# Logits of a unit's first block moved into the next unit, last scaling split in thirds, branch order changed, in a fused WKV and two-layer expert kernel

## The chip, the cores and the metric

The kernel runs as one launch on one core of a Trainium2 chip. The metric is the device time of the launch in microseconds (us), the median of the runs shown. A measurement of this kernel tells a change from none at about 0.5%.

## The reference

An attention part (a recurrence over 768 positions, two batches, eight heads of 48) makes 1536 tokens of 384 numbers. Two expert layers follow, each with 8 experts of width 1024. In both a token goes to the expert with the largest logit, and its result is scaled with that expert's softmax weight:

```
logits = x @ w_gate (+ modality bias, layer 0 alone)
e      = argmax(logits);  gate = softmax(logits)[e]
out    = gate * (relu(x @ w1[e]) @ w2[e])
```

Layer 1 reads layer 0's output. It also drops tokens beyond a capacity per expert. Its logits, `x @ w_gate` of layer 0's output, are made inside layer 0 as each block of results is finished.

## The kernel before, in words

**Units.** After the attention, `routing` sorts the tokens by expert into blocks of 128 and pairs the blocks into units of 256 with one expert each. `moe` then runs unit after unit: `body(j)` for j = 0 to 5 always, then `rest(j)`, which branches on the number of units that there are. With these inputs layer 0 has 8 units and layer 1 has 10. A unit with two blocks runs `two(j, pc)`, one with a single block runs `one(j, pc)`; `body` chooses with a branch on a register, `kd`, which every engine loads for itself. The form that stands second in the branch is reached by a jump.

**Work of a unit.** All products are made in three passes of float32r parts (high by high, high by low, low by high). `first2` makes a quarter of the hidden layer (18 matmuls of 256 columns, lines 1106), ScalarE and VectorE split it into `hh` and `hl` (lines 1111, 1112); `second2` adds a quarter to the output of one block (6 matmuls of 384 columns, line 1124). Between these stand `split` calls: ScalarE casts the next unit's weights to a high part (`hi`, line 965) and VectorE takes the low part (`lo`, line 968), ten pieces in all. `xprep` transposes the next unit's tokens (line 1024) and splits them (lines 1025, 1026). `gates` makes the softmax weight: part 0 on VectorE (lines 1033, 1034), part 1 an exponential on ScalarE (line 1036), part 2 on VectorE (1039, 1040). `scale(j, t)` multiplies the output of block t by it (line 1132).

**Logits of layer 0's output.** `yturn3` transposes a scaled block (line 1145), `ysplit3` splits it into three bf16 parts in the one buffer `yp` (1147 to 1152), and `ylog3` makes the logits with nine matmuls of 24 columns (line 730), reduces them (731) and stores the block with an indirect DMA. Of units 1 to 7 block 0's logits end the unit itself: `yturn3(j, 0)` stands between `second2(1, 1)` and `second2(2, 1)`, `ylog3(j, 0)` behind `second2(3, 1)`. Of unit 0 they stand in unit 1. Block 1's logits are made in the following unit.

**Order.** The order is written out by hand (`manual_schedule`); every engine runs its queue in program order, and its sequencer, which waits, loads registers and branches, runs ahead of it as far as no wait stops it. Inside `one` the order comes from the strings `ONE`: each letter is a step (a to j a piece of weights, y, z, l the logits of the block before, 0 and 1 the relus, Q part 2 of the gates, s the last scaling).

**End of layer 0.** `last(7)` is reached by a jump over the code of units 8 to 12. It transposes the last block (`yturn`, line 694), copies it, makes its logits (line 704), adds them to the logits that the other blocks stored, and layer 1's `routing` begins. While no product can run, `warm` keeps TensorE busy with matmuls of constants, 512 columns each (line 762): lists of 4 and 12 in the routing, 2 behind it, then 15 and 4 around the first unit's transposes.

Of the kernel before, what the change touches and what calls it, by code (L numbers as in the profile page):

```python
# [9 lines left out]
F32 = mybir.dt.float32  # L10
# [18 lines left out]
P = 128  # L29
# [14 lines left out]

WARM = (4, 12, 2, 15, 4)
TP = (3, 4)
OHP = ((0, 6), (6, 10), (10, 12))
# [21 lines left out]
SCALE = 'ssv'  # L69
LATE = (1,)  # L70
RELU = "sv"
PB = (1, 3, 1, 2)
ONE = (('ecadfyz', '01bQ', 'X', 'l', 'hgix', 'js'), ('badec0', 'f1hQ', 'xX', 'i', 'j', 'g'))

# [614 lines left out]

def turn3(tc, c, ap, psum, xt, n, tag, bufs):  # L690
    nc = tc.nc
    pt = psum.tile([P, KD, P], F32, tag=tag, name="lpt" + n, bufs=bufs)
    for kc in range(KD):
        nc.tensor.transpose(pt[:, kc], xt[:, kc * P : (kc + 1) * P], c.ident)
    xT = ap.tile([P, KD, P], F32, tag="lxT", name="lxT" + n, bufs=1)
    nc.scalar.copy(xT, pt)
    return [xT[:, kc] for kc in range(KD)]


def logits(tc, psum, xT, wg, dst, bias, n, tag, bufs):  # L700
# [58 lines left out]

def warm(nc, c, ps, k):  # L760
    for _ in range(k):
        nc.tensor.matmul(ps, lhsT=c.ones, rhs=c.i1.rearrange("p a b -> p (a b)")[:, 0:512].bitcast(BF16), start=True, stop=True)


def routing(tc, c, g, rp, layer, lg, cap, best, run, pick=None, bad=None, inside=None):
# [4 lines left out]
    with ExitStack() as ctx:  # L770
# [17 lines left out]
        pw = bank("warm0", "h", [P, 512])  # L788
        warm(nc, c, pw, WARM[0])
        nc.tensor.matmul(pc[:, 1], lhsT=c.blk, rhs=tot, start=False, stop=True, skip_group_check=True)  # L790
        nc.tensor.matmul(pc[:, 0], lhsT=c.tri, rhs=tot, start=True, stop=True, skip_group_check=True)
        warm(nc, c, pw, WARM[1])

# [48 lines left out]
        for col in range(NC):  # L842
            nc.tensor.matmul(pid, lhsT=ohp[:, :, col], rhs=rid[:, col], start=(col == 0), stop=(col == NC - 1))
        warm(nc, c, pw, WARM[2])
        R.ids = rp.tile([P, NB], I32, name="ids" + n)
# [89 lines left out]
class MoePools:  # L935
    def __init__(self, tc, ctx, raw, run):
        self.cp = cp = ctx.enter_context(tc.tile_pool(name="mo_c" + run, bufs=1, reuse_waits="tile"))
        self.ap = ctx.enter_context(tc.tile_pool(name="mo_p" + run, bufs=2, reuse_waits="tile"))

        def slots(nm, shape, dt, k=2):  # L940
            return [cp.tile(shape, dt, name=f"{nm}{i}") for i in range(k)]

        self.raw = raw
        self.w1r, self.w2r = raw.w1r, raw.w2r
        self.w1h = slots("w1h", [P, KD, F], F32R)
        self.w1l = slots("w1l", [P, KD, F], F32R)
        self.w2h = slots("w2h", [P, KF, DM], F32R)
        self.w2l = slots("w2l", [P, KF, DM], F32R)
        self.xg = slots("xg", [P, 2, XW], F32)
        self.xh = slots("xh", [P, KD, U], F32R)  # L950
        self.xl = slots("xl", [P, KD, U], F32R)
        self.yo = slots("yo", [P, 2, XW], F32)
        self.yp = cp.tile([P, 3, KD, P], BF16, name="yp")
        tc.nc.gpsimd.memset(self.yp, 0.0)
        self.gd = slots("gd", [P, 2, E + 1], F32)
        self.gm = cp.tile([P, 2, 2], F32, name="gm")


def moe(tc, c, m, route, run, layer, src, w1d, w2d, dst, wg2, wp2, zb, following, lgs=None, psum=None, bad=None, general=None, ykeep=None):
# [21 lines left out]
    with ctx:  # L981
# [133 lines left out]
        def second2(j, q, t, between=None):  # L1115
            s = j % 2
            hh, hl = st["t", j, q]
            if q == 0:
                st["y", j, t] = ykeep[t]
            ts = slice(t * P, t * P + P)  # L1120
            i = 0
            for (a, w) in ((hh, m.w2h), (hh, m.w2l), (hl, m.w2h)):
                for f in range(2):
                    nc.tensor.matmul(st["y", j, t], lhsT=a[:, f, ts], rhs=w[s][:, 2 * q + f], start=(q == 0 and i == 0), stop=(q == 3 and i == 5))  # L1124
                    i += 1
                    if i == 2 and between:
                        between()

# [28 lines left out]

        def yturn(j, t):
            st["yT", j, t] = turn3(tc, c, ap, psum, m.yo[j % 2][:, t], f"_y{j}{t}" + n, "tp", TP[layer])

        def ylog(j, t, out=True):
            pl = logits(tc, psum, st.pop(("yT", j, t)), wg2, m.yo[j % 2][:, t, DM:XW] if out else None, None, f"_y{j}{t}" + n, "lg", 1)
            if out:
                store(j, t)
            return pl

        def own(j, k):
# [11 lines left out]
        def one(j, pc):  # L1179
# [3 lines left out]
            def work():  # L1183
                for p in next(plan):
# [3 lines left out]
                    elif p == "y":  # L1188
                        if before:
                            if j == 1:  # L1190
                                ylog3(0, 0)
                            yturn3(j - 1, 1)
# [3 lines left out]
                    elif p == "l":  # L1196
                        if before:
                            ylog3(j - 1, 1)
                    elif p == "Q":
                        gates(j, 2)  # L1200
                    elif p == "s":
                        if layer == 0:
                            scale(j, 1, "s")
# [31 lines left out]
        def two(j, pc):  # L1235
            before = layer == 0 and j > 0
            first2(j, 0)
            if before:
                if j == 1:
                    ylog3(0, 0)  # L1240
                yturn3(j - 1, 1)
                ysplit3()
            own(j, 0)
            if j or layer:
# [13 lines left out]
            if j or layer:  # L1258
                split(pc, 6, 10)
            else:  # L1260
                split(pc, 3, 6)
            second2(j, 0, 1)
            first2(j, 3)
            if j == layer == 0:
                split(pc, 6, 8)
            second2(j, 1, 0)
            second2(j, 2, 0)
            if layer == 0:
                second2(j, 3, 0)
                scale(j, 0, SCALE[1])  # L1270
            if j + 1 < NU:
                for t in range(2):
                    xprep(j + 1, t)
            if layer:
                second2(j, 3, 0)
                scale(j, 0, SCALE[1])
            if j == layer == 0:
# [5 lines left out]

            second2(j, 1, 1)
            if layer == 0 and j:
                turned()
            second2(j, 2, 1)
            second2(j, 3, 1, turned if j == layer == 0 else None)
            if layer == 0:
                if j:  # L1290
                    ylog3(j, 0)
                scale(j, 1, "s")

        def body(j):
            pc = pieces(m, j + 1) if j + 1 < NU else []
            gates(j, 0)
            gates(j, 1)
            loads(j + 2)
# [8 lines left out]
            if j and layer:  # L1307
                finish(j - 1)
            if layer == 0 and j == NU_MIN - 1:

# [14 lines left out]
        for i in range(6) if layer == 0 else ():  # L1325
            lo(p0[i], nc.vector)
        warm(nc, c, psum.tile([P, 512], F32, tag="h", name="warm" + n, bufs=2), WARM[3])
        st["k"] = kind(0)
        xprep(0, 1)
        warm(nc, c, psum.tile([P, 512], F32, tag="h", name="warm1" + n, bufs=2), WARM[4])  # L1330
        for kc in range(KD):
# [8 lines left out]
        def last(j):  # L1340
            if layer:
                finish(j)
            else:
# [11 lines left out]
                m.raw.load(j % 2, *following, slice(er, er + 1), parts=(1,))  # L1355
                yturn(j, 1)
                py = ylog(j, 1, False)
                nc.vector.tensor_tensor(put, py.unsqueeze(1).to_broadcast((P, NC, E)), ohc.unsqueeze(2).to_broadcast((P, NC, E)), ALU.mult)
# [151 lines left out]
```

## Time and profile before

| what | value |
|---|---|
| median of three runs | 459.4 us (457.96 to 459.79) |
| the profiled execution's own time | 457.46 us |
| its span, first to last instruction | 455.4 us |
| TensorE busy (matmul) | 420.0 us, 92% of the span |
| VectorE busy | 330.4 us, 73% |
| ScalarE busy | 248.2 us, 55% |
| GpSimd busy | 142.6 us, 31% |
| mean granted TensorE clock | 0.985 |

The attention takes the first 112 us or so of the span, layer 0 runs from there to about 278, layer 1 to the end. Busy shares are means over all of it. A row of the timeline gives start and length in us, engine, line, operation and operands, how many were merged (x), and in brackets how long the engine was idle before it and which engine's signal ended that. Matmuls are pipelined: a merged row lasts longer than it holds up the next, which then starts before the row's end.

### The profile page before, as it was taken

What the parts mean: (1) busy time and instruction counts of PE and PEld (TensorE: products, weight loads), DVE (VectorE), ACT (ScalarE), POOL (GpSimd) and SP (SyncE); (2) the same over time, 40 slices, a digit from 0 to 9 for tenths busy, and PEclk for the clock granted to TensorE, in tenths of its full rate; (3) what the DMA queues carried; (4) which work ended last, traced back from release to release, by engine and by line L of the source; (5) the groups of instructions that cost most, each with busy time, mean ns of one, the idle gap of its engine ahead of it and who ended that gap; (6) DMA issues with size and microseconds to landing.
All of it is one profiled execution on the core that took longest, in us unless ns stands there. A gap on an engine that the chain in (4) does not pass through costs nothing. (4 is left out here: it accounts for less than half of the span.)

```text
span 455.4 us, 9522 instructions
## 1 busy us (share of the span) xinstructions
PE 420.0 (92%) x3212; PEld 376.5 (83%) x3212; DVE 330.4 (73%) x677; ACT 248.2 (55%) x504; POOL 142.6 (31%) x158
## 2 busy tenths in 40 slices
PE   8999999998899999999898976999899999998990
PEld 4789988886399989899897863699799999997990
DVE  7798777984888948677686895487874945868760
ACT  3356545544456646556374670277754755777650
POOL 5647953150330321212232220503343123124420
PEclk9999999999999999999999997999999999999997
DMA  5996247268520230357652855304886656762100
GB/s 113 197 157 132 52 80 197 43 223 304 172 73 2 72 94 19 108 159 243 215 185 64 304 188 157 89 21 142 285 285 248 240 185 232 234 223 55 46 22 19
DMA packets 85588, 66.95 MB, mean 147 GB/s; under 512 B 60586, under 2 KB 77655, under 8 KB 85504
## 3 DMA queue, kind: packets, MB, share of 16 engines
q1 hardware_dynamic: 80512, 52.30, 39.0%
q0 software_dynamic: 4992, 13.61, 9.4%
q8 instruction: 42, 0.69, 0.6%
q14 instruction: 42, 0.34, 0.2%
HBM read 95.63 MB, written 11.56 MB: 235 GB/s over the span
## 5 line engine op out<-in xcount | busy, mean ns | idle before, releaser
L968 DVE TENSOR_TENSOR w1l<-w1r,w1h 128x512 fp32r<-128x512 f32 x114 | 71.8, 686 | 13.7 <-ACT w1h L965 13.7
L968 DVE TENSOR_TENSOR w2l<-w2r,w2h 128x768 fp32r<-128x768 f32 x76 | 68.3, 951 | 0.1
L965 ACT CAST w1h<-w1r 128x512 fp32r<-128x512 f32 x114 | 62.8, 619 | 1.3 <-issue 1.0
L1112 DVE SCALAR_TENSOR_TENSOR qhl_m<-qh_m,qhh_m 128x512 fp32r<-128x512 f32 x48 | 32.9, 686 | 39.4 <-ACT qhh_m L1111 39.4
L965 ACT CAST w2h<-w2r 128x768 fp32r<-128x768 f32 x76 | 58.3, 834 | 0.0
L1106 PE MATMUL qh_m<-xh,w1h 128*128 128x256 f32 x288 | 51.4, 287 | 3.4 <-ACT yo L1132 3.1
L1106 PE MATMUL qh_m<-xl,w1h 128*128 128x256 f32 x288 | 50.3, 283 | 0.9 <-DVE w2l L968 0.7
L1124 PE MATMUL y_m<-w2h,qhh_m 128*128 128x384 f32 x192 | 50.4, 344 | 0.0
L1124 PE MATMUL y_m<-w2h,qhl_m 128*128 128x384 f32 x192 | 49.6, 339 | 0.8 <-DVE qhl_m L1112 0.7
L1106 PE MATMUL qh_m<-xh,w1l 128*128 128x256 f32 x288 | 49.8, 282 | 0.0
L1124 PE MATMUL y_m<-w2l,qhh_m 128*128 128x384 f32 x192 | 49.2, 337 | 0.0
L1111 ACT ACTIVATE qhh_m<-qh_m 128x512 fp32r<-128x512 f32 x48 | 28.7, 598 | 33.3 <-PE qh_m L1106 33.3
L1137 POOL DMA_INDIRECT x<-yo,ids_l x14 | 17.3, 1236 | 93.7 <-ACT w2h L965 33.1
L1009 POOL DMA_INDIRECT xg<-x,idg_l x24 | 24.6, 1025 | 69.4 <-DVE gd L1034 44.5
L1106 PEld LDWEIGHTS qh_m<-xh,w1h 128*128 128x128 f32 x288 | 42.3, 188 | 4.2 <-ACT yo L1132 3.4
L1106 PEld LDWEIGHTS qh_m<-xl,w1h 128*128 128x128 f32 x288 | 41.0, 188 | 1.5 <-DVE w2l L968 1.1
L1132 ACT ACTIVATE yo<-y_m,gate_l 128x384 f32<-128x384 f32 x30 | 17.5, 582 | 43.1 <-PE y_m L1124 40.1
L1106 PEld LDWEIGHTS qh_m<-xh,w1l 128*128 128x128 f32 x288 | 40.9, 188 | 0.0
L1137 POOL DMA_INDIRECT out_dram<-yo,ids_l x20 | 24.1, 1203 | 49.5 <-ACT w1h L965 13.9
L1124 PEld LDWEIGHTS y_m<-w2h,qhl_m 128*128 128x128 f32 x192 | 34.4, 188 | 2.4 <-DVE qhl_m L1112 2.4
L1009 POOL DMA_INDIRECT xg<-xs,idg_l x20 | 22.0, 1102 | 43.7 <-issue 21.1
L395 ACT ACTIVATE X<-endt,Sb 112x112 f32<-112x112 f32 x40 | 14.2, 354 | 38.2 <-PE endt L385 27.2
(250 smaller groups left out, 868.7 us busy)
## 6 DMA issues: line engine op xcount, KB each, us to landing
w2r<-in_moe_w_dram SPq DMA_DIRECT2D x50, 768.0 KB
w1r<-in_moe_w_dram SPq DMA_DIRECT2D x72, 512.0 KB
xs<-zv SPq DMA_DIRECT2D x12, 192.0 KB
out_dram<-zt SPq DMA_DIRECT2D x4, 576.0 KB
raw_w<-in_w_dram SPq DMA_DIRECT2D x14, 144.0 KB
raw_r<-in_r_dram SPq DMA_DIRECT2D x14, 144.0 KB
raw_k<-in_k_dram SPq DMA_DIRECT2D x14, 144.0 KB
raw_v<-in_v_dram SPq DMA_DIRECT2D x14, 144.0 KB
```

Of the source, the lines that this page charges most:

```text
L395: nc.scalar.activation(Xn, z, AF.Identity, scale=Tn)
L965: (eng.copy if eng is nc.scalar else eng.tensor_copy)(p[1], p[0])
L968: eng.tensor_sub(p[2], p[0], p[1].bitcast(F32))
L1009: nc.gpsimd.indirect_dma_start(out=m.xg[j % 2][:, t], out_offset=None, in_=src, in_offset=bass.IndirectOffsetOnAxis(ap=R.idg[:, 2 * j + t ...
L1106: nc.tensor.matmul(ph[:, f], lhsT=w[s][:, kc, fs], rhs=a[s][:, kc], start=(i == 0), stop=(i == 3 * KD - 1))
L1111: nc.scalar.activation(hh, ph, AF.Relu)
L1112: nc.vector.scalar_tensor_tensor(hl, ph, 0.0, hh.bitcast(F32), ALU.max, ALU.subtract)
L1124: nc.tensor.matmul(st["y", j, t], lhsT=a[:, f, ts], rhs=w[s][:, 2 * q + f], start=(q == 0 and i == 0), stop=(q == 3 and i == 5))
L1132: nc.scalar.activation(m.yo[j % 2][:, t, 0:DM], py, AF.Identity, scale=R.gate[:, 2 * j + t : 2 * j + t + 1])
L1137: nc.gpsimd.indirect_dma_start(out=dst, out_offset=bass.IndirectOffsetOnAxis(ap=R.ids[:, 2 * j + t : 2 * j + t + 1], axis=0), in_=m.yo[j % ...
```

## The change

- `two`: of units 0 to 4 (`NU_MIN` is 6) block 0 is transposed inside `second2(2, 1)`, behind its second matmul, and `ylog3(j, 0)` moves to the following unit, behind `first2(0)`. From unit 5 on it is transposed inside `second2(1, 1)` behind the fourth matmul, and `ylog3` stands inside `second2(3, 1)` behind the fourth. In layer 0 `xprep` moves ahead of `second2(3, 0)`, as it was in layer 1. The tenth piece of weights is split behind `first2(3)`.
- Part 1 of the gates moves from `body` into the forms: behind `first2(0)` in `two`, letter P in `one`.
- The scaling of block 1 moves out of `two` and `one` for units 5 and up of layer 0, into `body(j + 1)` ahead of its branch, or into `last`, where it is made in three parts of 128 columns, each with its own transposition and copy.
- The form `one` stands first in the branch for units 6 and 7 and no longer for unit 5.
- Three of the five `warm` lists run in layer 1 as four times as many matmuls of 128 columns.
- Block 0 of both buffers `yo` is cleared once on GpSimd, before layer 0.

```diff
+WIDE = ((512, 512, 512, 512, 512), (512, 512, 128, 128, 128))
+ONE_FIRST = (6, 7)
-ONE = (('ecadfyz', '01bQ', 'X', 'l', 'hgix', 'js'), ('badec0', 'f1hQ', 'xX', 'i', 'j', 'g'))
+ONE = (('ecadfPyz', '01bQ', 'X', 'l', 'hgix', 'js'), ('badec0P', 'f1hQ', 'xX', 'i', 'j', 'g'))
...
+def warm(nc, c, ps, i, layer):
+    w = WIDE[layer][i]
+    for _ in range(WARM[i] * 512 // w):
+        nc.tensor.matmul(ps[:, 0:w], lhsT=c.ones, rhs=c.i1.rearrange("p a b -> p (a b)")[:, 0:w].bitcast(BF16), start=True, stop=True)
...
+        for x in self.yo:
+            tc.nc.gpsimd.memset(x[:, 0], 0.0)
...
-                            if j == 1:
-                                ylog3(0, 0)
+                            if j < NU_MIN:
+                                ylog3(j - 1, 0)
...
                     elif p == "s":
-                        if layer == 0:
+                        if layer == 0 and j < NU_MIN - 1:
                             scale(j, 1, "s")
...
+            gates(j, 1)
             own(j, 0)
...
-                split(pc, 6, 10)
+                split(pc, 6, 9)
...
+            else:
+                split(pc, 9, 10)
             second2(j, 1, 0)
             second2(j, 2, 0)
-            if layer == 0:
-                second2(j, 3, 0)
-                scale(j, 0, SCALE[1])
             if j + 1 < NU:
                 for t in range(2):
                     xprep(j + 1, t)
-            if layer:
-                second2(j, 3, 0)
-                scale(j, 0, SCALE[1])
+            second2(j, 3, 0)
+            scale(j, 0, SCALE[1])
...
-            second2(j, 1, 1)
-            if layer == 0 and j:
-                turned()
-            second2(j, 2, 1)
-            second2(j, 3, 1, turned if j == layer == 0 else None)
-            if layer == 0:
-                if j:
-                    ylog3(j, 0)
+            end = layer == 0 and j >= NU_MIN - 1
+            second2(j, 1, 1, (turned, 4) if end else None)
+            second2(j, 2, 1, (turned, 2) if layer == 0 and not end else None)
+            second2(j, 3, 1, (lambda: ylog3(j, 0), 4) if end else None)
+            if layer == 0 and not end:
                 scale(j, 1, "s")
...
             gates(j, 0)
-            gates(j, 1)
...
             if j and layer:
                 finish(j - 1)
-            if layer == 0 and j == NU_MIN - 1:
+            elif j >= NU_MIN:
+                scale(j - 1, 1, "s")
+            if layer == 0 and j in ONE_FIRST:
...
-                yturn(j, 1)
-                py = ylog(j, 1, False)
+                for kc in range(KD):
+                    ks = slice(kc * P, kc * P + P)
+                    nc.scalar.activation(m.yo[j % 2][:, 1, ks], ykeep[1][:, ks], AF.Identity, scale=R.gate[:, col])
+                xT = ap.tile([P, KD, P], F32, tag="lxT", name=f"lx{j}" + n, bufs=1)
+                for kc in range(KD):
+                    pt = psum.tile([P, P], F32, tag="h" if kc == 1 else "tp", name=f"yt{j}{kc}" + n, bufs=2 if kc == 1 else TP[0])
+                    nc.tensor.transpose(pt, m.yo[j % 2][:, 1, kc * P : (kc + 1) * P], c.ident)
+                    nc.scalar.copy(xT[:, kc], pt)
+                py = logits(tc, psum, [xT[:, kc] for kc in range(KD)], wg2, None, None, f"_y{j}1" + n, "lg", 1)
```

## Rows read from the trace of the kernel before

**Rows 1.** Waits of TensorE, 120 to 290 us: total us, times, longest.
```profile
PE qh_m L1106 <- ACT yo L1132: 3.1, 4, 1.0
PE hp_m L1077 <- DVE h_m L1070: 1.6, 2, 1.0
PE hp_m L1077 <- ACT h_m L1068: 1.5, 1, 1.5
PE ph_m L1058 <- ACT yo L1132: 1.2, 1, 1.2
```
**Rows 2.** Timeline, TensorE, the end of unit 1.
```profile
163.35 0.51 PE L1124 MATMUL y_m<-w2h,qhl_m 128*128 128x384 f32 x2
163.70 0.52 PE L730 MATMUL l_y_m<-wp,yp 128*128 128x24 bf16 x9
164.96 0.36 PE L1106 MATMUL qh_m<-xh,w1h 128*128 128x256 f32 x1 [0.74 <-ACT yo L1132]
```
**Rows 3.** Timeline, TensorE and ScalarE, the end of unit 0.
```profile
144.07 0.52 PE L1106 MATMUL qh_m<-xh,w1h 128*128 128x256 f32 x3
145.15 0.39 PE L1106 MATMUL qh_m<-xl,w1h 128*128 128x256 f32 x1 [0.20 <-DVE yp L1151]
...
144.27 0.58 ACT L1132 ACTIVATE yo<-y_m,gate_l 128x384 f32<-128x384 f32 x1 [0.16 <-PE y_m L1124]
```
**Rows 4.** TensorE's branches of `body`, 163.6 to 165.1, then 141 to 144 us.
```profile
L1316 PEldq COMPARE_BRANCH  x2: 65/176/286, 164.0 to 164.7; - x2
...
L1316 PEldq COMPARE_BRANCH  x2: 65/192/319, 141.2 to 142.0; - x2
```
**Rows 5.** Timeline, TensorE and VectorE, unit 2's last quarter.
```profile
178.81 0.52 PE L1124 MATMUL y_m<-w2l,qhh_m 128*128 128x384 f32 x2
179.53 0.62 PE L1124 MATMUL y_m<-w2h,qhl_m 128*128 128x384 f32 x2 [0.20 <-DVE qhl_m L1112]
...
176.19 2.69 DVE L968 TENSOR_TENSOR w2l<-w2r,w2h 128x768 fp32r<-128x768 f32 x3
```
**Rows 6.** Timeline, ScalarE and VectorE, the start of unit 7.
```profile
260.44 0.22 ACT L1036 ACTIVATE gd<-gd 128x16 f32<-128x16 f32 x1 [0.96 <-DVE gd L1034]
261.28 1.14 ACT L965 CAST w1h<-w1r 128x512 fp32r<-128x512 f32 x2 [0.62 <-issue]
...
261.99 0.69 DVE L968 TENSOR_TENSOR w1l<-w1r,w1h 128x512 fp32r<-128x512 f32 x1 [1.58 <-ACT w1h L965]
```
**Rows 7.** Timeline, ScalarE and TensorE, the end of layer 0.
```profile
270.83 0.84 ACT L965 CAST w2h<-w2r 128x768 fp32r<-128x768 f32 x1
272.58 0.58 ACT L1132 ACTIVATE yo<-y_m,gate_l 128x384 f32<-128x384 f32 x1 [0.91 <-PE y_m L1093]
275.31 0.48 ACT L696 COPY lxT_y_m<-lpt_y_m 128x384 f32<-128x384 f32 x1 [2.15 <-DVE sp_m L1350]
...
275.84 1.45 PE L704 MATMUL lpl_y_m<-wg,lxT_y_m 128*128 128x8 f32 x6 [1.84 <-ACT lxT_y_m L696]
```
**Rows 8.** TensorE's branch into `last`, 269 to 276 us; then all of the span.
```profile
L1380 PEldq COMPARE_BRANCH  x1: 3407/3407/3407, 269.8 to 269.8; - x1
...
L1380 PEldq COMPARE_BRANCH  x10: 65/66/4684, 246.1 to 446.0; - x10
```
**Rows 9.** The page's groups: ScalarE's scaling of 112 columns, in the attention.
```profile
L395 ACT ACTIVATE X<-endt,Sb 112x112 f32<-112x112 f32 x40 | 14.2, 354 | 38.2 <-PE endt L385 27.2
```
**Rows 10.** Timeline, TensorE: layer 1's warm matmuls and transposes; nine short matmuls.
```profile
286.44 3.40 PE L762 MATMUL warm_m<-i,ones 128*128 128x512 bf16 x15
289.68 0.49 PE L1024 MATMUL xp_m<-ident,xg 128*128 128x128 f32 x3
...
146.68 0.39 PE L730 MATMUL l_y_m<-wp,yp 128*128 128x24 bf16 x9
```
**Rows 11.** Layer 1: timeline, VectorE, start of unit 2; waits of TensorE.
```profile
322.91 0.69 DVE L968 TENSOR_TENSOR w1l<-w1r,w1h 128x512 fp32r<-128x512 f32 x1 [1.67 <-ACT w1h L965]
...
PE qh_m L1106 <- DVE w2l L968: 0.7, 2, 0.4
```

More of the change, by code (lines that the diff above doesn't have):

```diff
@@ L687, in attention_general @@
             nc.sync.dma_start(xs[b * S + j * P : b * S + (j + 1) * P, DM:XW], lg[:, col])
[L690 to L697, printed above, removed]
 def logits(tc, psum, xT, wg, dst, bias, n, tag, bufs):
@@ L757, in steps @@
         yield v.scalar_tensor_tensor(self.oh[:, :, a:z].rearrange("p e c -> p c e"), cum, 1.0, eq, ALU.is_equal, ALU.mult)
-def warm(nc, c, ps, k):
-    for _ in range(k):
-        nc.tensor.matmul(ps, lhsT=c.ones, rhs=c.i1.rearrange("p a b -> p (a b)")[:, 0:512].bitcast(BF16), start=True, stop=True)
+def warm(nc, c, ps, i, layer):
+    w = WIDE[layer][i]
+    for _ in range(WARM[i] * 512 // w):
+        nc.tensor.matmul(ps[:, 0:w], lhsT=c.ones, rhs=c.i1.rearrange("p a b -> p (a b)")[:, 0:w].bitcast(BF16), start=True, stop=True)
 def routing(tc, c, g, rp, layer, lg, cap, best, run, pick=None, bad=None, inside=None):
@@ L788, in routing @@
         pw = bank("warm0", "h", [P, 512])
-        warm(nc, c, pw, WARM[0])
+        warm(nc, c, pw, 0, layer)
         nc.tensor.matmul(pc[:, 1], lhsT=c.blk, rhs=tot, start=False, stop=True, skip_group_check=True)
         nc.tensor.matmul(pc[:, 0], lhsT=c.tri, rhs=tot, start=True, stop=True, skip_group_check=True)
-        warm(nc, c, pw, WARM[1])
+        warm(nc, c, pw, 1, layer)
         nb = T("nb", [P, E], I32)
@@ L843, in routing @@
             nc.tensor.matmul(pid, lhsT=ohp[:, :, col], rhs=rid[:, col], start=(col == 0), stop=(col == NC - 1))
-        warm(nc, c, pw, WARM[2])
+        warm(nc, c, pw, 2, layer)
         R.ids = rp.tile([P, NB], I32, name="ids" + n)
@@ L1125, in second2 @@
                     i += 1
-                    if i == 2 and between:
-                        between()
+                    if between and i == between[1]:
+                        between[0]()
         def scale(j, t, eng):
@@ L1156, in ylog3 @@
             store(j, t)
[L1158 to L1165, printed above, removed]
         def own(j, k):
@@ L1198, in work @@
                             ylog3(j - 1, 1)
-                    elif p == "Q":
-                        gates(j, 2)
+                    elif p == "P" or p == "Q":
+                        gates(j, 1 + (p == "Q"))
                     elif p == "s":
-                        if layer == 0:
+                        if layer == 0 and j < NU_MIN - 1:
                             scale(j, 1, "s")
@@ L1238, in two @@
             if before:
-                if j == 1:
-                    ylog3(0, 0)
+                if j < NU_MIN:
+                    ylog3(j - 1, 0)
                 yturn3(j - 1, 1)
                 ysplit3()
+            gates(j, 1)
             own(j, 0)
@@ L1326, in moe @@
             lo(p0[i], nc.vector)
-        warm(nc, c, psum.tile([P, 512], F32, tag="h", name="warm" + n, bufs=2), WARM[3])
+        warm(nc, c, psum.tile([P, 512], F32, tag="h", name="warm" + n, bufs=2), 3, layer)
         st["k"] = kind(0)
         xprep(0, 1)
-        warm(nc, c, psum.tile([P, 512], F32, tag="h", name="warm1" + n, bufs=2), WARM[4])
+        warm(nc, c, psum.tile([P, 512], F32, tag="h", name="warm1" + n, bufs=2), 4, layer)
         for kc in range(KD):
```

## The prediction, as it went on record

> **What bounds the kernel now.** I read the waits of TensorE first, then the timeline around each of the places that they name. In layer 0 TensorE is the bound: inside a unit its matmuls stand without a gap, and what it loses, it loses at the seams. The list shows three kinds: the first product of a unit, put down to the last scaling (3.1 us over four seams, 1.2 at the fifth, where unit 6 begins), and two waits for the hidden layer in the one-block units 6 and 7 [rows 1]. The timeline adds two: a short stall in the last quarter of units 2 to 5, four in count [rows 5], and the end of layer 0, where nothing else runs [rows 7]. One correction holds for every wait: a merged row lasts about 0.16 us longer than it holds up the next (163.35 + 0.51 against 163.70 [rows 2]), so an idle time of 0.74 costs about 0.90.
>
> The rows name ScalarE's last scaling as what ends the wait at the seam. I don't believe it. Unit 0 ends with the same scaling, and there TensorE begins the next unit at 144.07, before that scaling has even begun at 144.27 [rows 3]. The difference is where TensorE's own sequencer stands. At the end of unit 0 it has its two branches behind it at 142.0, two microseconds before the first product; at the end of unit 1 they come at 164.0 and 164.7 and the product at 164.96 [rows 2, 4]. What holds it there is `ylog3`: its last three matmuls wait for the third bf16 part, the nine take 0.52 us [rows 2] where an undisturbed set takes 0.39 [rows 10], and only then does the sequencer get to the branch, with nothing queued to cover it.
>
> **The change part by part.**
>
> *Seams of units 1 to 4.* `ylog3` leaves the end of the unit, the last wait is then at the transposition, with ten matmuls behind it (1.75 us at 0.175 each, two in 0.35 by [rows 2]), so branch and register load are covered as at the end of unit 0. The nine matmuls are not saved, only moved. Gain: 3.1 + 4 x 0.16 + 4 x 0.13 for the wait inside `ylog3` = 4.25. If the scaling were the cause after all, all of it stays and the nine matmuls (0.23 each set without their own tail) come on top, 0.9 lost. The stores move to the next unit with the logits; GpSimd then issues the gather of two units ahead before the store and not behind it, which delays nobody.
>
> *Last quarter, units 2 to 5.* VectorE is in three low parts in a row until 178.9, so the split of the last quarter is late and TensorE waits 0.20 and takes 0.62 instead of 0.52 for the next two [rows 5]: 0.46 each, 1.85 in four. The change takes the third piece (about 0.9) behind that split and puts six transposes before the matmul that waits. Either alone covers 0.46. What is late next is the scaling of block 0, now behind the copies of `xprep`; it has eight matmuls, 1.4 us, before its transposes, and needs 0.7. Bounds 1.0 to 1.85.
>
> *Into unit 6.* `ylog3` stays at the end here, but with two matmuls behind it, so 0.35 of the 1.2 are covered; the branch at the end of `two` that now has to jump over the other form takes some back. 0.3, between 0 and 0.6. In unit 6 the wait for the hidden layer, 0.5 (1.6 less 1.0 [rows 1]) plus 0.16, goes because ScalarE's casts no longer stand behind the exponential: 0.7. Together 1.0, between 0.4 and 1.5.
>
> *Unit 7.* ScalarE ends the scaling at 259.5, then waits 0.96 for VectorE's first part of the gates, and after the exponential another 0.62 for its load and jump; its first cast is at 261.28 and VectorE, free since 260.4, starts at 261.99 [rows 6]. With the exponential behind the fifth cast and the form standing first, the cast begins at about 259.5. VectorE then starts as soon as it is through its own branch: of its 1.58 I leave 0.43 for that (an estimate by TensorE's steps at the seam, whose branches lie 0.7 apart [rows 4]). VectorE has no gap from there to the relu that TensorE waits for, so the unit ends 1.15 earlier, of 2.5 that are lost there [rows 1]. Between 0.6 and 2.7.
>
> *End of layer 0.* Before: ScalarE's scaling at 272.58, its jump, the copy at 275.31, the logits at 275.84, six matmuls in 1.45 [rows 7], end 277.29. The branch is issued as soon as the instruction before it has started, so the jump took 2.7. Now that instruction is the cast at 270.83, and ScalarE is in `last` at 273.5, TensorE at 273.2 (269.8 + 3.4 [rows 8]). Three scalings, by the nearest row 0.35 each (112 columns [rows 9]), end at 274.5 to 274.6, the transposes lag by one; three copies at about 0.27 (my estimate, between a third of the 0.48 of [rows 7] and 0.35) end at 275.4, and the first logits can start with the first copy at 274.9. They are through at 276.2. Gain 1.1. If the jump begins only with the cast's end it is nothing; if the jump were free, 2.0.
>
> *Layer 1, units of one block.* Two of them follow one of the same form, and VectorE waits 1.67 there for the first cast, which stands behind exponential and scaling [rows 11]. As in unit 7 about 1.0 of it goes, less 0.15 for the exponential that now stands among the casts: 0.85 in each. TensorE waits for VectorE's end of those units [rows 11]; with its smaller waits for the relu it can use most. The two one-block units ahead of them only get the later exponential, 0.15 lost each. Net 1.2, between 0 and 1.6.
>
> *Warm matmuls of layer 1.* Fifteen of 512 columns take 3.40 us and the transposes stand right behind, so their length is on the path [rows 10]: 0.216 each, 54 ns per 128 columns, the weight load hidden. As 76 of 128 (60 and 16) they cost nothing more if the load stays hidden. The nine short ones go at (0.39 - 0.16) / 8 = 28 ns for load and 24 columns; if load and columns add up, 82 ns each, 2.1 us lost. I take 0.15, near the lower end, because the long pairs show the load hidden.
>
> The Trainium skill, "TensorE: Matmul & The Clock Gate", section "Back-to-back issue gap", speaks against this edit: it gives about 81 ns per matmul for a stream of pairs at 128 columns, against 56 for the isolated gap. By 81 the edit would lose 2.05, by 56 it would lose 0.15. The same section says 131 ns at 512 columns; the 216 of the fifteen does not agree, which is why I don't give it more weight.
>
> *The rest.* The two clears of `yo` stand on GpSimd long before its first gather; the exponential moved in the two-block units costs ScalarE nothing that TensorE sees.
>
> Sum: 4.25 + 1.85 + 1.0 + 1.15 + 1.1 + 1.2 - 0.15 = 10.4. The profiled execution took 457.46 (455.4 of span and 2.06 around it), below all three runs; the median is 459.4. I count from half way, 458.4: **448.0 us**.
>
> **The rivals.**
>
> *The scaling is what the seam waits for*, as the rows say. Then the seams give nothing and lose 0.9: 458.4 - (10.4 - 4.25 - 0.9) = 453.2. For it: the named releaser, and units 1 to 4 keep their scaling at the end. Against: the end of unit 0. Chance 0.08.
>
> *A new wait takes the seam's place.* At the end of unit 0 the third group of products waits for the chain that splits the transposed block (144.07 to 145.15, where six matmuls take 0.70 and no gap: 0.4 to 0.45 [rows 3]). If each of the four new seams gets it, 1.8 is lost: 449.8. Against it: VectorE is late in unit 0 because of weight pieces that the later units don't have there. 0.12.
>
> *The short warm matmuls pay for their weights*: 1.95 more, 450.0. 0.12.
>
> *The jump into `last` is no earlier*: 449.1. 0.05.
>
> *Slower: the jumps.* Every seam's branch now skips the other form, and what covers it is the 1.75 of matmuls plus 0.33 of transposes behind the last wait, less 1.0 for the steps themselves (164.0 to 164.96 [rows 2, 4]): 1.1 to spare. Branches of 0.3 are covered. But the same kind of branch has taken 3.4 and 4.7 us on TensorE where its target was far [rows 8]. At 3.4, 2.0 would show at each of six seams, 12 us: 460.0; at 4.7, 3.3 each: 467.8. It turns the sign from about 3.1 us a branch on. Against it: the branches at all four seams before were near ones. 0.03.
>
> **How the numbers follow.** The forecast has 0.60; its own range is 446 to 450.5. The rivals above hold 0.40. The range is 444.5 to 452.0: the lower end is the sum of the better bounds at unit 7, layer 0's end and unit 6 (3.0 more) and a start from the profiled time, the upper leaves out the first and the last rival. Within 0.5% means 457.1 to 461.7: only the jumps, or several terms failing together, lead there. Faster 0.94, same 0.03, slower 0.03.
>
> **What would show it.** TensorE's waits: no row of `qh_m` behind `yo` at units 2 to 5, first products less than 0.2 us behind the last second-layer matmul, the branches more than 1 us ahead of it. No wait of `y_m` for `qhl_m`. The first cast of unit 7 right behind a scaling. In `last`, the copy of a third less than 2 us behind the last product of unit 7. The 60 short matmuls in 3.2 to 3.5 us. The prediction is wrong if the seams still show 0.6 or more, or if the 60 take 4.5.

## The result, and the profile after

| kernel | median, us | runs | to before |
|---|---|---|---|
| before | 458.72 | 457.96 to 459.79, 5 runs | |
| changed | 451.99 | 451.07 to 452.46, 5 runs | 0.9849, 95% interval 0.9828 to 0.9869 |

The changed kernel is faster, at the upper edge of the range and 4 us above the 448.0 that I gave. The profiled execution took 451.07 (span 449.3, mean granted clock 0.979) against 457.46 (455.4, 0.985): 6.14 of span gained where the sum said 10.4.

The first matmul of each stage, read from both traces, divides this (us; plus is gain):

| stage | before | after | forecast | measured |
|---|---|---|---|---|
| up to layer 0's first product | 125.84 | 126.82 | 0 | -0.98 |
| units 1 to 6, first product to first product | 114.64 | 107.24 | 7.1 | 7.40 |
| unit 7 | 13.50 | 12.27 | 1.15 | 1.23 |
| last product of layer 0 to layer 1's routing | 6.62 | 9.12 | 1.1 | -2.50 |
| routing to layer 1's first product | 12.71 | 13.85 | -0.15 | -1.14 |
| layer 1's ten units | 151.97 | 149.68 | 1.2 | 2.29 |
| behind the last product | 11.91 | 12.06 | 0 | -0.15 |

A product's time is its start. Unit 0 is unchanged. The units gave what was forecast and a little more. What is missing lies between them, in the end of layer 0 above all: 3.6 us. A second profile of before, on another chip (before_again, run 5), has 116.80 for units 1 to 6 and 14.85 for unit 7, so the two gains in the table are those of one pair of profiles.

TensorE's waits of the changed kernel, 115 to 285 us (total, times, longest), to be held against [rows 1]:

```profile
PE yt_m L1347 <- ACT yo L1343: 2.8, 1, 2.8
PE lpl_y_m L696 <- issue: 2.5, 1, 2.5
...
PE hp_m L1072 <- DVE h_m L1065: 1.6, 1, 1.6
PE ph_m L1053 <- ACT yo L1127: 0.7, 1, 0.7
```

The four waits for `yo` at the starts of units 2 to 5 are gone, and of three waits for the hidden layer one is left. New is the second line: 2.5 us for which the trace names no releaser ("issue").

The seam from unit 1 to unit 2, TensorE's timeline and its two branches there, answers to [rows 2, 4]. The last products run into the first without a gap, though the scaling stands where it stood, and the branches come at 161.7 and 162.4, 1.8 us ahead of the product instead of 0.26:

```profile
163.53 0.51 PE L1119 MATMUL y_m<-w2l,qhh_m 128*128 128x384 f32 x2
163.88 0.51 PE L1119 MATMUL y_m<-w2h,qhl_m 128*128 128x384 f32 x2
164.22 0.52 PE L1101 MATMUL qh_m<-xh,w1h 128*128 128x256 f32 x3
...
L1300 PEldq COMPARE_BRANCH  x2: 65/176/286, 161.7 to 162.4; - x2
```

In unit 2 the low-part products that took 0.62 with a wait of 0.20 [rows 5] take 0.51 and wait for nothing. At the start of unit 7 the first cast stands right behind the scaling, answering to [rows 6] (ScalarE's timeline):

```profile
179.28 0.51 PE L1119 MATMUL y_m<-w2h,qhl_m 128*128 128x384 f32 x2
...
252.49 0.58 ACT L1127 ACTIVATE yo<-y_m,gate_l 128x384 f32<-128x384 f32 x1 [0.90 <-PE y_m L1088]
252.97 0.61 ACT L960 CAST w1h<-w1r 128x512 fp32r<-128x512 f32 x1
```

The end of layer 0, ScalarE and TensorE, and TensorE's branch into `last`, answers to [rows 7, 8]:

```profile
263.23 0.84 ACT L960 CAST w2h<-w2r 128x768 fp32r<-128x768 f32 x1
267.15 0.88 ACT L1343 ACTIVATE yo<-y_m,gate_l 128x128 f32<-128x128 f32 x3 [3.09 <-DVE w2l L963]
268.08 0.64 ACT L1348 COPY lx_m<-yt_m 128x128 f32<-128x128 f32 x3
...
264.05 0.86 PE L1088 MATMUL y_m<-w2h,hl_m 128*128 128x384 f32 x4
267.75 0.67 PE L1347 MATMUL yt_m<-ident,yo 128*128 128x128 f32 x3 [2.85 <-ACT yo L1343]
270.92 1.24 PE L696 MATMUL lpl_y_m<-wg,lx_m 128*128 128x8 f32 x6 [2.49 <-issue]
...
L1372 PEldq COMPARE_BRANCH  x1: 4701/4701/4701, 262.9 to 262.9; - x1
```

The reader is to see two things. The jump took 4.70 instead of 3.41. And the first copy of a third, issued at 268.08, was long done when the logits began at 270.92.

Layer 1's start answers to [rows 10]; below it are the instruction packets among the DMAs from the second gather's issue to the second set of transposes, of the changed kernel:

```profile
281.34 3.51 PE L755 MATMUL warm_m<-i,ones 128*128 128x128 bf16 x60
284.69 0.50 PE L1019 MATMUL xp_m<-ident,xg 128*128 128x128 f32 x3
286.78 0.55 PE L1317 MATMUL xp_m<-ident,xg 128*128 128x128 f32 x3 [0.70 <-DMA xg<-x,idg_l]
...
q0 software_dynamic: 173, 0.56, 52.1%
q8 instruction: 1, 0.02, 1.5%
```

The 60 short matmuls took what was forecast; the second gather is late.

### The profile page after: what moved, and what is told of

Read it like the earlier page. It is cut to its first block, busy times and chain, and to the rows that moved or that the text cites. A ratio compares the mean times of both kernels' runs of the same rounds, so it can differ in the third digit from the quotient of the medians.

```text
span 449.3 us, 9663 instructions
## 1 busy us (share of the span) xinstructions
PE 417.9 (93%) x3270; PEld 380.1 (85%) x3275; DVE 329.5 (73%) x677; ACT 249.3 (55%) x508; POOL 143.3 (32%) x160
## 5 line engine op out<-in xcount | busy, mean ns | idle before, releaser
L963 DVE TENSOR_TENSOR w2l<-w2r,w2h 128x768 fp32r<-128x768 f32 x76 | 69.2, 951 | 0.3 <-ACT w2h L960 0.3
L960 ACT CAST w2h<-w2r 128x768 fp32r<-128x768 f32 x76 | 59.4, 835 | 0.0
L1004 POOL DMA_INDIRECT xg<-x,idg_l x24 | 26.0, 1083 | 69.2 <-DVE gd L1029 43.3
L1132 POOL DMA_INDIRECT out_dram<-yo,ids_l x20 | 22.1, 1103 | 49.3 <-ACT w2h L960 11.5
L1020 ACT CAST xh<-xp_m 128x384 fp32r<-128x384 f32 x38 | 16.7, 485 | 35.8 <-PE xp_m L1019 35.8
```

The lines of the kernel that those rows point to most:

```text
L960: (eng.copy if eng is nc.scalar else eng.tensor_copy)(p[1], p[0])
L963: eng.tensor_sub(p[2], p[0], p[1].bitcast(F32))
L1004: nc.gpsimd.indirect_dma_start(out=m.xg[j % 2][:, t], out_offset=None, in_=src, in_offset=bass.IndirectOffsetOnAxis(ap=R.idg[:, 2 * j + t ...
L1020: nc.scalar.copy(m.xh[j % 2][:, :, ts], pt)
L1132: nc.gpsimd.indirect_dma_start(out=dst, out_offset=bass.IndirectOffsetOnAxis(ap=R.ids[:, 2 * j + t : 2 * j + t + 1], axis=0), in_=m.yo[j % ...
```

## The experiments

The runs stood on several chips, so times are compared by their ratio to before, or stage by stage.

**1. Where TensorE's code stands.** In the whole span queue q8 brings TensorE 44 packets, 0.72 MB: 16 KB each. My theory was that the wait of 2.5 us is for such a packet. Layer 0's code exists twice (the second copy, for a general case, isn't executed); matmuls in a ninth unit that never runs move everything behind them:

```diff
             with tc.If(nblk > j) as cmp:
+                if layer == 0 and j == NU_MIN + 2:
+                    pt = psum.tile([P, 512], F32, tag="h", name="pad" + n, bufs=2)
+                    for _ in range(16):     # pad_q1; 32 in pad_q2, 64 in pad_q4
+                        nc.tensor.matmul(pt[:, 0:128], lhsT=c.ones, rhs=..., start=True, stop=True)
                 body(j)
```

> The changed kernel with 32 bf16 matmuls of 128 columns put into two copies of a unit that is not executed (16 in each), so that all TensorE code behind it, the end of layer 0 and layer 1, stands 64 instructions (4 KB, a quarter of the 16 KB that one instruction packet of TensorE brings) later. What is executed is the same. Theory A (the 2.49 us that TensorE loses between the transposes and the first logits at the end of layer 0 is the wait for its next packet of instructions, because the packet ends some nine instructions into that code): the packet now ends beyond it, the wait is under 0.4 us, last product of layer 0 to first logits 3.9 us instead of 6.35, time about 449.5. Theory B (the four engines' jumps, all issued within 1.5 us, and the DMAs there hold each other up): nothing moves, 6.3 us and 452.0.

> The same with 64 such matmuls (32 in each copy), 128 instructions, half a packet. Theory A: as with a quarter, the wait of the first logits under 0.4 us and about 449.5 in all; where the packet of instructions falls in layer 1's start moves too, so its second gather, which landed 4.07 us after its issue in the changed kernel and 3.01 in the kernel before, may land about 1 us earlier. Theory B: 452.0.

> The same with 128 such matmuls (64 in each copy), 256 instructions, one whole packet: the code stands as far into its packet as in the changed kernel. Theory A: the wait of 2.5 us is there, last product to first logits 6.3 us, 452.0. If the wait goes here as well, the place in the packet isn't the cause, and moving the code at all is; theory B: 452.0.

Measured: pad_q1 450.1 (0.9742, 0.9713 to 0.9771), pad_q2 449.38 (0.9731, 0.9703 to 0.9760), pad_q4 453.53 (0.9815, 0.9782 to 0.9848), all on one chip. From last product to first logits 4.08, 4.45 and 7.42. TensorE's waits of pad_q4 at the end of layer 0, then its timeline in pad_q2:

```profile
PE yt_m L1347 <- issue: 3.8, 1, 3.8
PE lpl_y_m L696 <- issue: 2.7, 1, 2.7
```
```profile
268.00 0.80 PE L1347 MATMUL yt_m<-ident,yo 128*128 128x128 f32 x3 [3.46 <-ACT yo L1343]
268.65 0.89 PE L696 MATMUL lpl_y_m<-wg,lx_m 128*128 128x8 f32 x6
```

A quarter or half a packet takes the wait away and a whole one brings it back: theory A. The packets' own records agree. While TensorE waits in the changed kernel, one q8 packet is under way (DMAs, 268.2 to 269.8):

```profile
q8 instruction: 1, 0.02, 5.4%
```

It lands at 269.66 and the logits begin 1.26 us later; in pad_q4 and in after_again (run 5) they begin 1.38 and 1.44 behind such a landing. The same work is 4.2 us apart by the place of its code alone (pad_q4 against pad_q2). B can't tell pad_q2 from pad_q4 and falls for this wait; the jump stays at 4.68 to 4.92 in all three.

**2. The turn in one again**, on the base of pad_q2:

```diff
-            if layer == 0 and not end:
+            if layer == 0:
                 scale(j, 1, "s")
...
-                for kc in range(KD):     # three scalings, then three transposes, each with its copy
+                for kc in range(KD):
+                    nc.tensor.transpose(pt[:, kc], m.yo[j % 2][:, 1, kc * P : (kc + 1) * P], c.ident)
+                nc.scalar.copy(xT, pt)
```

> The changed kernel, code moved by half a packet as in pad_q2, and the end of layer 0 as in the kernel before: the last block is scaled in one at the unit's end, ahead of ScalarE's jump, and turned with three transposes and one copy. Against pad_q2 this prices the turn by thirds without the wait for instructions. If the thirds are worth what was forecast, this is 1.1 us slower than pad_q2 (450.6 if that is 449.5). If ScalarE's jump takes about 2.7 here (issued 1.6 us after the others) and 4.0 in pad_q2, and TensorE's and VectorE's are shorter too, the jumps hold each other up, and the thirds are worth under 0.5 us.

452.15 (0.9779, 0.9745 to 0.9813), 2.8 above pad_q2. From last product to first logits 6.36 against 4.45, but 1.3 of that is TensorE's branch out of unit 7, 1.83 here and 0.53 there, which held up the jump's issue. That leaves 0.6 for the thirds, under the 1.1. ScalarE's jump, issued 0.8 us behind VectorE's, took 4.3, about as long as in pad_q1 (4.4); what makes the jumps long is tried in run 4. Units 5 and 6 lost 0.6 each; unit 5's isn't the edit's, since the unit is as long (21.10) in one_first6_q2 and wide512_q2 (21.11 and 21.17), which don't touch it.

**3. The seams.** The logits back at the end of units 1 to 4:

```diff
-                if j < NU_MIN:
-                    ylog3(j - 1, 0)
+                if j == 1:
+                    ylog3(0, 0)
...
-            second2(j, 1, 1, (turned, 4) if end else None)
+            second2(j, 1, 1, (turned, 4) if end else (turned, 6) if back else None)
...
+            if back:
+                ylog3(j, 0)
```

> The changed kernel with the logits of each first block put back to the end of units 1 to 4 (and the transposes with them, between the second and third group), as in the kernel before; scaling, split order and all else as changed. By itself this moves the code of layer 0's end to 145 instructions ahead of the end of its packet, so it compares with pad_q2 (449.4), not with the changed kernel. Theory S (TensorE's sequencer gets to its branches only behind the logits, whose third part comes late): units 2 to 5 begin with a gap of 0.7 to 0.9 again, with the scaling named as releaser, 4.2 us over the four, 453.6. Theory R (the scaling itself is what the next unit waits for, as the rows of before say): the gaps are the same with the logits at either place, 449.4 or a little less, since the logits then stand once less beside the next unit's start.

462.16 (0.9981, 0.9951 to 1.001). By the ratios that is 0.025 above pad_q2 (0.9731), some 11.5 us and nearly all that pad_q2 had gained; the 12.7 of a later expectation is a difference of times from two chips. TensorE's waits, 115 to 262 us, and its branches out of units 6 and 7:

```profile
PE ph_m L1053 <- issue: 4.4, 1, 4.4
PE qh_m L1101 <- ACT yo L1127: 2.8, 4, 0.8
...
L1298 PEldq COMPARE_BRANCH  x1: 6387/6387/6387, 253.1 to 253.1; - x1
L1298 PEldq COMPARE_BRANCH  x1: 3640/3640/3640, 270.1 to 270.1; - x1
```

The four seams are back with the scaling named, and cost 4.26 (units 1 to 4 by their first products, against pad_q2). TensorE's two branches stand close ahead of the product again; that of unit 3 begins at 184.49:

```profile
L1303 PEldq COMPARE_BRANCH  x2: 65/178/290, 183.5 to 184.3; - x2
```

The rest is branches. The 6.39 of unit 6's branch end 1.40 us behind the landing of a q8 packet, as the waits of run 1 do. That branch jumps over the two-block form, 304 instructions. By my count in the compiled program, which no trace shows, with a packet's border where run 1 showed one, it here goes from place 213 of a packet to place 5 of the next but one; in the changed kernel from 25 to 73 of the next, and takes 0.30. To have the edit without that I put matmuls that never run into unit 5's other form and the ninth unit:

> seam_back (the logits of the first block at the end of units 1 to 4 again) with matmuls that are never executed put in, 32 into the one-block form of unit 5 and 16 into each copy of the ninth unit, so that units 6 and 7 and the end of layer 0 stand where they stand in the changed kernel and pad_q1, to within six instructions. seam_back lost 12.7 us against pad_q2, 4.26 of them at the four seams, 4.7 at the start of unit 7, where TensorE's branch at the end of unit 6 took 6.39 us instead of 0.30, and 2.5 at layer 0's end, where the branch of unit 7 took 3.64. Theory L (those are the place of the code and not the edit): here they are gone, the branch at the end of unit 6 takes 0.3, and the time is 4.3 us above pad_q2_again. If they belong to the edit: 12 us above.

455.25 (0.9908, 0.9873 to 0.9943), 8.6 above pad_q2_again (446.67) and not 4.3. The same view of it:

```profile
PE qh_m L1101 <- ACT yo L1127: 2.8, 4, 0.8
...
L1298 PEldq COMPARE_BRANCH  x3: 68/394/2185, 252.7 to 265.3; - x3
```

The seams cost 4.30, and unit 6's branch is back at 0.4: L for that part. What is over that stands, in its profile, at the branch out of unit 7 (2.19, first logits 1.8 later), in layer 1's routing and gather (1.4) and at a branch of layer 1 that took 4.23 (1.7 on its unit). I had not lined those of layer 1 up. Both branches waited for code: they end 1.41 and 1.39 us behind the landing of a q8 packet. The place of unit 7's branch is that of pad_q1, and there it took 0.40, so place alone doesn't set it. In pad_q1 the q8 packet ahead of it began 2.8 us before the branch, here 0.2; why so late, no run shows.

**4. The jump.** On the base of pad_q2:

```diff
-ONE_FIRST = (6, 7)
+ONE_FIRST = (6,)
```

> The changed kernel with the one-block form first in unit 6 alone, not in unit 7, code moved by half a packet as in pad_q2. Unit 7 then jumps over the two-block form on its way in and has nothing to jump over on its way out. Theory J (in the changed kernel TensorE's branch at the end of unit 7 has to fetch code, 16 KB at 0.7 us behind that branch, and the fetch for the jump into the end of layer 0 queues behind it): that jump, 4.7 to 4.9 us long, goes back to 3.4, last product to first logits from 4.4 to about 3.2, and unit 7's first cast comes about 0.6 later: 448.8 against pad_q2's 449.4. Theory K (the jumps are long because four engines jump within 1.5 us): the jump stays at 4.7 or more, unit 7 loses 0.6, 450.0.

454.1 (0.9809, 0.9776 to 0.9842), slower than pad_q2 (0.9731), and yet J. TensorE's branch into `last`, its timeline there, and its branch into unit 7:

```profile
L1372 PEldq COMPARE_BRANCH  x1: 3785/3785/3785, 266.1 to 266.1; - x1
...
270.10 0.71 PE L1347 MATMUL yt_m<-ident,yo 128*128 128x128 f32 x3 [1.21 <-ACT yo L1343]
270.75 0.83 PE L696 MATMUL lpl_y_m<-wg,lx_m 128*128 128x8 f32 x6
...
L1300 PEldq COMPARE_BRANCH  x1: 5392/5392/5392, 250.1 to 250.1; - x1
```

From last product to first logits 2.20: 1.44 less than before's 3.64. VectorE's and GpSimd's jumps fell with TensorE's, from 3.9 and 4.3 in pad_q1 to 3.0 and 2.8, though all four were issued about as close together (within 1.9 us, 1.7 in pad_q1). ScalarE's fell too, from 4.4 to 2.6, but it is 2.5 in pad_q4 beside a TensorE jump of 4.80. seam_back says it more plainly: there the four stand 2.9 us apart, as in before (2.8), and TensorE's took 4.73. So K falls. But unit 7's branch, 0.9 us behind unit 6's, took 5.39 and cost 3.9, where I had 0.6; it ends 1.40 behind a q8 packet's landing. That miss is the prediction's own slower rival: a branch to code that hasn't been brought yet.

**5. The warm matmuls.** On the base of pad_q2:

```diff
-WIDE = ((512, 512, 512, 512, 512), (512, 512, 128, 128, 128))
+WIDE = ((512, 512, 512, 512, 512), (512, 512, 512, 512, 512))
```

> The changed kernel with layer 1's warm matmuls all of 512 columns again, code moved by half a packet. By my term for them 0.15 us faster than pad_q2. In the profiles of pad_q1, pad_q2 and pad_q4 the 60 short ones run at 56 ns each up to the fiftieth and then stall four times for 0.5 us with nothing shown that they wait for, and from the gather of layer 1 to its first unit it takes 7.9 to 8.0 us, against 6.2 in the changed kernel's profile and 5.1 before. Theory W (so many short instructions in a row outrun what brings TensorE its instructions): here that stretch takes 5.1 to 6.2 and the time is 447.2 to 448.0. Theory G (the gather itself lands late there): it stays at 7 or more, time 449.3.

> The kernel before, unchanged, for a second profile of it, beside these runs. Theory W: from the gather of layer 1 to its first unit 5.1 us as in its first profile. Theory G: 7 us or more. The granted clock at layer 0's start (119 to 123 us), half in the changed kernel's profile, in pad_q2 and in tail_old_q2 and full in the first profile of before, in pad_q1 and in pad_q4: either, if it goes by the execution and not by the kernel.

wide512_q2: 448.76 (0.9694, 0.9663 to 0.9725). The stretch from the issue of layer 1's first gather to its first product is 5.12 there, 5.13 in before_again (463.23 in its one run), and 7.99 in pad_q2 with the short ones. TensorE's timeline of pad_q2 there:

```profile
279.25 3.10 PE L755 MATMUL warm_m<-i,ones 128*128 128x128 bf16 x50
282.79 0.27 PE L755 MATMUL warm_m<-i,ones 128*128 128x128 bf16 x2 [0.43 <-issue]
283.50 0.27 PE L755 MATMUL warm_m<-i,ones 128*128 128x128 bf16 x2 [0.44 <-issue]
```

So it isn't the gather (G), but the changed kernel's own trace shows no such stall. On one chip:

> The changed kernel, unchanged, beside the next three on one chip. Theory A: the wait of 2.5 us for instructions at the end of layer 0 is there again, and it is 2.5 to 4 us slower than pad_q2_again. Against before as measured first, 0.985.

> pad_q2 a second time, as the base for the next two. Theory A: no wait over 0.5 us between the last transposition and the first logits, 0.973 of before.

> pad_q2 with layer 1's warm matmuls of 512 columns, a second time, now on the same chip as pad_q2. In the profiles so far, the stretch from layer 1's gather to its first unit is 5.1 with these and 7.9 to 9.3 with the short ones. Theory W (the short ones cost this in every execution): 1.5 to 3 us faster than pad_q2_again in the timed runs, which is the rival of the prediction that put 1.95 on them. Theory P (the stalls come with the recording of a profile: SyncE's semaphore instructions stall for 0.55 to 0.69 us in the same stretch): the runs without a profile differ by less than 0.5 us.

after_again 450.35 (0.9806, 0.9769 to 0.9844), pad_q2_again 446.67 (0.9726, 0.9690 to 0.9763), wide512_q2_again 447.37 (0.9743, 0.9705 to 0.9780). The changed kernel is 3.7 us slower than pad_q2, as theory A had it (2.5 to 4), and its profile has the wait for code again (1.9, in pad_q2_again none). Here the short ones don't stall (TensorE's timeline of pad_q2_again), and the stretch is 5.23 against 5.08 with long ones:

```profile
279.29 3.51 PE L755 MATMUL warm_m<-i,ones 128*128 128x128 bf16 x60
282.64 0.50 PE L1019 MATMUL xp_m<-ident,xg 128*128 128x128 f32 x3
```

That is the 0.15 of the forecast. W doesn't hold everywhere: on this chip the short ones are 0.7 us faster in the median, inside the uncertainty. Whether the stalls on the two other chips are there without a profile stays open; pad_q2's ratio is the same on a chip with them (0.9731) and without (0.9726), which speaks for P.

These runs bear on the late gather too. From issue to landing the second one took 3.01 before, 4.07 and 4.33 in the two profiles of the changed kernel, 3.11 in pad_q2_again. In the two late ones a packet of instructions stands among its rows (q8 in the fence on layer 1's start); in the other two there is none. In seam_back_aligned the packet stands in the first gather, which took 3.90 where those four profiles have 3.10 to 3.19; the second, issued just ahead of the packet, took 3.04. So a packet goes with one late gather each time, and not always with the second.

They also settle the first stage: before_again has TensorE's granted clock at half (1.2 GHz of 2.4) from 119.6 us on, as the changed kernel has, and its first profile hadn't. Windows of before_again, then of the changed kernel (the columns are busy times, then TensorE's granted clock):

```profile
119.70:123.00 3.30, 3.24 (x9) 1.08 (x8) 3.06 (x16) 0.00 (x0) 1.97 (x2) 0.50 0.13 23
```
```profile
119.00:123.40 4.40, 4.34 (x19) 1.82 (x19) 3.77 (x19) 0.00 (x0) 2.40 (x3) 0.61 0.17 46
```

So it goes by the execution; the 0.98 is not the change's.

## Why the prediction was right and where it was wrong

*The sum.* 6.1 of the 10.4 came, and the time stands 0.01 us inside the upper end of the range: that the range holds it is luck. Its lower end, by its own terms, is 444.1 and not 444.5; nothing hangs on that.

*Seams.* Right, in mechanism and size: 4.25 forecast, 4.26 and 4.30 by putting the logits back. The first rival, the scaling as the releaser, falls: the scaling stayed and the gaps went.

*Last quarter.* Right in size where it was forecast: counted from the start of one product to the start of the next, the second-layer products of units 2 to 4 take 9.04 to 9.05 in before and 8.62 to 8.63 in seam_back_aligned, 0.42 each against 0.46. Units 1 to 4 together are 2.2 shorter there than before even with the logits at the end; the rest of that is unit 1 (0.49, half of it a stall at the same place that I had left out) and a seam of unit 4 that was longer in before (0.4). The new wait of the second rival is nowhere in the list: units 1 to 4 take 18.88 to 19.17 each.

*Units 5 to 7.* Unit 7 is right in mechanism and size: 1.15 against 1.23, with VectorE's wait of 1.58 [rows 6] down to 0.41, where I had left 0.43. Unit 6 gave 0.60 of 0.7. Unit 5, up to unit 6's first product, gave 0.37, where its last quarter and the seam behind it stand with 0.46 and 0.3. So the 7.40 of units 1 to 6 comes near 7.1 in part by chance: units 1 to 4 gave 0.8 more than their terms (6.41 against 5.63), units 5 and 6 0.5 less.

*Layer 1's units.* 1.2 forecast, 2.29 measured. VectorE's wait [rows 11] fell from 1.67 to 0.49, where I had taken 1.0 off (its timeline, the same place):

```profile
317.77 1.90 DVE L963 TENSOR_TENSOR w1l<-w1r,w1h 128x512 fp32r<-128x512 f32 x3 [0.49 <-ACT w1h L960]
```

The one-block units behind gained 1.25 and 1.10, and those ahead, for which I had 0.15 lost each, lost 0.14 and 0.15.

*Warm matmuls.* Right: 60 in 3.51 and 0.15 lost, on chips without the stalls. The Trainium skill, "TensorE: Matmul & The Clock Gate", section "Back-to-back issue gap", has 81 ns for a stream of these; the trace stays with its isolated 56. What made this stage 1.14 longer was the late gather.

*End of layer 0.* This is the step that failed: "TensorE at 273.2 (269.8 + 3.4)" and logits "with the first copy at 274.9". It took the jump from the trace of before and let the code behind it run at once. From the last product's start to the first logits that makes 2.70; it took 6.35. Of the 3.65 between, 2.49 are the wait for code and 1.29 the longer jump. Another 0.73 is that TensorE's branch goes out later (1.68 ahead of the last product's start instead of 2.41), since the branch over the other form (0.63) now stands ahead of it; and from TensorE's arrival to the logits it took 0.86 less than I had, the wait left out. The rival that the jump is no earlier doesn't explain it: ScalarE's branch went out 1.55 us ahead of the last product's start, before 0.38 behind it. Its jump grew too, from 2.7 to 4.1, so the scalings begin 2.59 behind that start and not 1.3. So the copy of a third, which was to come less than 2 us behind the last product, came 3.5 behind its start. Run 1 removes the 2.49 without touching the work and run 4 most of the 1.29; with both gone the step gives 1.44, where I had 1.1.

The jump grew because the one-block form now stands first in unit 7 and its end jumps over the other form: run 4 takes that away. A packet of code is then brought just before the jump into `last` asks for its own. In the changed kernel two 16 KB packets stand on q8 in that jump, in before one (the DMAs from branch to arrival; the changed kernel first):

```profile
q8 instruction: 2, 0.03, 4.4%
```
```profile
q8 instruction: 1, 0.02, 1.8%
```

The packet that begins about 1 us behind the branch took 2.32 beside the other and 0.96 alone in before, 1.36 more, about what the jump grew by. That the two packets hinder each other is argued from this and not shown by itself.

The Trainium skill, "Runtime: NRT & Kernel Launch", section "Instruction fetch mechanics", says that a taken branch out of a window of two pages must wait for its page: the traces agree (0.30 against 6.39 for the same branch), as far as my count of places goes. It calls the cost of a page border mostly hidden; some nine instructions behind a jump it was 2.49.

*The slower rival* had the right thing and the wrong place: branches that must fetch cost 3.4 to 6.4, but in this kernel the seams' code happened to stand well. Nothing in my working said that it would; that it did is luck. seam_back and one_first6_q2 show what the same sort of edit costs where it doesn't.

The best versions measured are the changed kernel with half a packet of dead code in it: pad_q2 with 0.9731 and 0.9726 of before on two chips, and wide512_q2, which these runs don't tell from it, with 0.9694 and 0.9743. after_again has 0.9806 on the chip of the second of each.

## What to carry to other kernels

A far branch has a price of its own, and so has a border of instruction packets shortly behind one: look up what TensorE runs in the first microsecond after each jump, and what jumped just before it. An edit moves all code behind it, so a test that undoes it should keep the code in its place, or be read stage by stage; a few hundred dead instructions tell whether a wait marked "issue" is one for code, and so does holding its end against the landing of the engine's instruction packets. Read a wait's releaser against a second place in the trace where the same releaser is harmless: that is what found the seams.

## What was not expected of the hardware

- One and the same branch out of unit 6 took 0.30 and 6.39 us, with its code in another place.
- TensorE's waits for code end 1.26 to 1.53 us behind the landing of a 16 KB packet on q8: branches of 1.55, 1.83, 2.19, 3.64, 4.23, 5.39 and 6.39 us and the three waits at the first logits (1.95 to 2.73).
- Two fetches of code in TensorE's far jump went with longer jumps on VectorE and GpSimd: 2.9 to 3.0 and 2.8 to 3.3 with one, 3.8 to 4.8 and 3.5 to 4.9 with two, save in seam_back (2.8 and 3.0), where TensorE jumps last. ScalarE's take 2.5 to 4.8 with two, under 2.9 in five of eleven profiles.
- A 16 KB packet of instructions among a gather's rows went with 0.7 to 1.3 us on its landing (second gather: 3.01 and 3.11 without, 4.07 and 4.33 with; first: 3.10 to 3.19 without, 3.90 with).
- Sixty matmuls of 128 columns stalled three or four times, for 0.4 to 1.2 us, after the fiftieth in the profiles of two chips, and not at all in the changed kernel's first profile and in the three of a third chip.
